# Rest of a feed-forward in two sweeps, the second with seven products of quarter blocks in place of eight

## The chip, the cores and the metric

The kernel runs on one core of a Trainium2 chip. The metric is device time in microseconds (us). Engines: PE does matrix products (PEld is its loading of weights), DVE vector work, ACT activations and copies, POOL elementwise work, SP issues most transfers. Matrix products write to PSUM, which has eight banks of 128 x 512 32-bit words; all else lies in SBUF.

## The reference

`B=8` batches, `S=576` positions, `DM=512` (8 heads of 64), hidden width 2048; 4608 tokens in all.

```python
kv  = einsum('bhsd,bhse->bhde', k, v); out = einsum('bhsd,bhde->bhse', q, kv)
x   = out / sqrt(mean(out*out, -1) + 1e-6) * g_norm        # heads side by side: (8, 576, 512)
u   = x + real(fft(fft(x, axis=1), axis=2))
un  = (u - mean(u, -1)) / sqrt(var(u, -1) + 1e-6)
out = u + maximum(un @ w_ch1, 0) @ w_ch2                   # w_ch1 512x2048, w_ch2 2048x512, 64-bit
```

## The kernel before, in words

All large products take 32-bit operands split into a high word that PE multiplies exactly and a low word that holds the rest; each product is three matmuls (`passes`): high x high, high x low, low x high. The weights come as 64-bit numbers; `sum_w` turns 512 columns of them into 32-bit values (one ACT operation, five on DVE and an addition), `split_w` makes the two words (ACT rounds, POOL subtracts), and for the first weights also takes each column's mean out through a small matmul (`w_mean`).

The tokens are 9 blocks (`NBLK`) of 512 (`BT`), each of 4 tiles of 128. The hidden width is 16 chunks f of 128. For a block and a chunk there are two halves of work. `ffn1` (L350 to L361): 12 matmuls, weights `w` of chunk f against the transposed tokens `unTh`, `unTl`, 512 columns each, into a bank `ps_h`; ACT takes the relu rounded (`hh`, L364), DVE the low word (`hl`, L367). `ffn2` (L369 to L378): for each of four tiles 3 matmuls of 512 columns, `hh` or `hl` against the second weights, summed over f in a bank `acc` per tile. A row's factor 1/sqrt(var) is the same for a whole token and positive, so it is left out of the hidden values and multiplied in at the end.

The program has two parts. Up to L1051 a planner (class `Plan`) emits attention, Fourier transform, norm and chunks f = 0 to 2 of the feed-forward, in order of ranks; the partial sums go to memory (`part_scr`), u to `u_scr`, the transposed tokens to `unT_scr`. From there on, the rest of the feed-forward is written out in program order, and a scheduler places the instructions of each engine in its queue. It works in steps of one block and one chunk: `first` of this step, then `second` of the step before (so 12 and 12 matmuls of 512 columns), and beside it one unit of weight conversion and the loads ahead (`load_unT`, two transfers of 1024 KB a block; `load_parts`, `load_u`). Four blocks first run f = 3 to 6, whose weights are ready, and store sums to `next_scr`; then all nine blocks run what is left, while the 18 weight units of f = 7 to 15 are converted, one a step. When a block is complete, `load_u` has computed the factors of its rows (`rs_yb`) and put u and the partial sums together in `uu`; DVE adds `acc` times the factor (L1186), and SP stores the tile (L1189).

Of the kernel before, what the change touches and what calls it, by code (L numbers as in the profile page):

```python
# [27 lines left out]
NA = 3  # L28
NB1 = 4
# [156 lines left out]
def kernel(  # L186
# [74 lines left out]
    part_scr = dram.tile([NTOK, DM], F32, name="part_scr")  # L261
    next_scr = dram.tile([NTOK, DM], F32, name="next_scr")
    unT_scr = dram.tile([NBLK, P, 2, KC * BT], F32, name="unT_scr")
# [82 lines left out]
    def h_tile(name):  # L346
        return base.tile([P, BT], F32R, name=name, tag="r", bufs=RINGS["h"])
# [487 lines left out]
    def plan_w(which, f, pool, r, after=(), r_load=None):  # L835
        pair = {}

        def make():
            pair["t"] = pool().tile([P, 2, BT], F32R, name=f"w{which}{f}", **(
                dict(tag="wA", bufs=2 * NA) if f < NA else {}  # L840
            ))
            w_t[which, f] = (pair["t"][:, 0], pair["t"][:, 1])
# [214 lines left out]
    def craw(name):  # L1057
        return wA.tile([P, 2 * DM], F32, name=name, tag="wA", bufs=2 * NA)

# [15 lines left out]
    def sum_w(which, f):  # L1075
# [9 lines left out]
        sums[which, f] = af, pf[:, :P]  # L1085

    def split_w(which, f):
# [5 lines left out]
        pair = wB2.tile([P, 2, BT], F32R, name=f"w{which}{f}")  # L1093
        hi, lo = w_t[which, f] = (pair[:, 0], pair[:, 1])
        nc.scalar.activation(hi, af, AF.Copy)  # L1095
        nc.gpsimd.tensor_tensor(lo, af, hi.bitcast(F32), ALU.subtract)  # L1096

    F1 = NA + NB1
    early = [NBLK - 2, NBLK - 1] + list(range(NBLK - 3, NBLK - 1 - NSEG, -1))
    blocks = early[::-1][: len(early) - 2] + early[:2] + list(range(1, NBLK - NSEG)) + [0]  # L1100
# [3 lines left out]
    tiles_of = {j: list(range(TPB)) for j in blocks}  # L1104
    tiles_of[0] = [2, 3, 0, 1]
    acc_t = {}
# [4 lines left out]
    def load_parts(j):  # L1111
        parts[j] = []
        for i in range(TPB):
            n = j * TPB + i
            two_ = []
            for src in (part_scr, next_scr)[: 2 if j in early else 1]:
                part = upool.tile([P, DM], F32, name="up", tag="up", bufs=6)
                nc.sync.dma_start(part, src[n * P : (n + 1) * P])
                two_.append(part)
            if j in early:  # L1120
                nc.gpsimd.tensor_tensor(two_[0], two_[0], two_[1], ALU.add)
            parts[j].append(two_[0])

    def load_u(j):
        us[j] = []
        mv = tiny.tile([P, TPB, 2], F32, name="bmv")
        for i in range(TPB):
            n = j * TPB + i
            ut = upool.tile([P, DM], F32, name="uu", tag="uu", bufs=8)
            if ascending(n):  # L1130
# [15 lines left out]
        for i in range(TPB):  # L1146
# [5 lines left out]
            nc.gpsimd.tensor_tensor(us[j][i], us[j][i], part, ALU.add)  # L1152

    held = [NBLK - 2, NBLK - 1]

# [7 lines left out]
    def first(j, f):  # L1163
        ps = bank("ps_h")
        ffn1(ps, w_t[1, f], unTs[j])
        hh, hl = h_tile("hh"), h_tile("hl")
        relu_hi(hh, ps)
        relu_lo(hl, ps, hh)
        return hh, hl

    def second(seg, hpair, f):
        j, f0, f1 = seg
        for i in tiles_of[j]:
            if f == f0:
# [4 lines left out]
            t = j * TPB + i  # L1179
            if f1 < NF:  # L1180
                part = upool.tile([P, DM], F32, name="up", tag="up", bufs=6)
                nc.scalar.copy(part, acc_t[i])
                nc.sync.dma_start(next_scr[t * P : (t + 1) * P], part)
                continue
            ut = us[j][i]
            nc.vector.scalar_tensor_tensor(  # L1186
                ut, acc_t[i], scales[j][:, i : i + 1], ut, ALU.mult, ALU.add
            )
            nc.sync.dma_start(out[t * P : (t + 1) * P, :], ut)  # L1189

    prev = None
    step = 0
    for n, seg in enumerate(segs):
        j, f0, f1 = seg
        for f in range(f0, f1):
            if step == 0:
                load_w(*units[0])
                load_w(*units[1])
            if step + 2 < len(units):
                load_w(*units[step + 2])  # L1200
            if f == f0 and n + 1 < len(segs) and segs[n + 1][0] not in held:
                load_unT(segs[n + 1][0], j)
            hpair = first(j, f)
            if prev:
                second(*prev)
            prev = (seg, hpair, f)
            if 0 < step <= len(units):
                split_w(*units[step - 1])
            if step < len(units):
                sum_w(*units[step])  # L1210
            step += 1
            if f == min(f0 + 2, f1 - 2):
                if f1 == NF:
                    load_parts(j)
                    load_u(j)
    second(*prev)
    late.close()
# [81 lines left out]
```

## Time and profile before

| | |
|---|---|
| median of 3 runs | 1027.12 us (1025.77 to 1027.71) |
| profiled execution | 1026.22 us, its span 1024.4 us |
| mean granted TensorE clock | 0.996 |
| busy: PE, PEld, DVE, ACT, POOL | 993.9, 839.4, 472.0, 322.4, 320.6 us |
| matmuls | 5866, of which 3456 at L354 and L372 have 512 columns |
| moved by transfers | 140.70 MB, 137 GB/s on average |

In a line of instructions the columns are: line, engine, operation, output <- inputs, shapes, count, then total busy time in us and the mean of one in ns, then the idle time of the engine just before them and what ended it. A busy share in a line of slices is given in tenths, 9 being 90% or more. Matmuls are pipelined: the mean of one is longer than the interval between two.

### The profile page before, as it was taken

What the parts mean: (1) busy time and instruction counts of PE and PEld (TensorE: products, weight loads), DVE (VectorE), ACT (ScalarE), POOL (GpSimd) and SP (SyncE); (2) the same over time, 40 slices, a digit from 0 to 9 for tenths busy, and PEclk for the clock granted to TensorE, in tenths of its full rate; (3) what the DMA queues carried; (4) which work ended last, traced back from release to release, by engine and by line L of the source; (5) the groups of instructions that cost most, each with busy time, mean ns of one, the idle gap of its engine ahead of it and who ended that gap; (6) DMA issues with size and microseconds to landing.
All of it is one profiled execution on the core that took longest, in us unless ns stands there. A gap on an engine that the chain in (4) does not pass through costs nothing.

```text
span 1024.4 us, 15026 instructions
## 1 busy us (share of the span) xinstructions
PE 993.9 (97%) x5866; PEld 839.4 (82%) x5866; DVE 472.0 (46%) x838; ACT 322.4 (31%) x655; POOL 320.6 (31%) x332
## 2 busy tenths in 40 slices
PE   4698999999999999999999999999999999999998
PEld 4697898889888888888888888888888888888886
DVE  4758775654588689998131314131221311311211
ACT  2456565555545434334221212021121021210110
POOL 0555876864865131225722303020020010110000
PEclk9998999999999999999999999999999999999999
DMA  9979979663246766645552515140320400400101
GB/s 245 253 164 280 190 214 263 168 182 139 88 162 212 275 206 253 228 136 175 155 177 74 182 51 170 71 139 1 125 81 0 165 21 1 164 1 1 42 1 41
DMA packets 109194, 140.70 MB, mean 137 GB/s; under 512 B 51790, under 2 KB 76418, under 8 KB 104516
## 3 DMA queue, kind: packets, MB, share of 16 engines
q1 hardware_dynamic: 105588, 132.28, 42.4%
q0 software_dynamic: 1920, 6.29, 2.0%
q10 hardware_dynamic: 1616, 1.18, 0.4%
q8 instruction: 46, 0.75, 0.3%
q14 instruction: 24, 0.20, 0.1%
HBM read 88.33 MB, written 51.40 MB: 136 GB/s over the span
## 4 chain that ended last, share of the span: by engine, by line
PE 93%; DMA 2%; DVE 2%; SPq 1%; issue 1%; ACT 0%; POOL 0%; DVEq 0%; ACTq 0%; POOLq 0%
PE ps_h L354 38%; PE acc L372 38%; PE ps_o L554 4%; PE ps_f L727 3%; PE ps_f L693 3%; PE ps_k L481 3%; PE ps_q L529 2%; PE ps_t L813 2%; DMA vm<-in_v_dram 2%; DVE x L651 1%; DMA qt<-in_q_dram 1%; SPq L510 1%; PE ps_w L315 0%; SPq L460 0%; DVE unTl L825 0%
## 5 line engine op out<-in xcount | busy, mean ns | idle before, releaser
L354 PE MATMUL ps_h<-unTh,w 128*128 128x512 f32 x1152 | 357.1, 391 | 0.0
L372 PE MATMUL acc<-w,hh 128*128 128x512 f32 x1152 | 345.0, 391 | 0.2 <-DVE unTl L825 0.2
L367 DVE SCALAR_TENSOR_TENSOR hl<-ps_h,hh 128x512 fp32r<-128x512 f32 x144 | 99.2, 689 | 379.8 <-ACT hh L364 377.5
L354 PEld LDWEIGHTS ps_h<-unTh,w 128*128 128x128 f32 x1152 | 215.4, 188 | 44.0
L372 PEld LDWEIGHTS acc<-w,hh 128*128 128x128 f32 x1152 | 214.9, 188 | 44.3 <-issue 0.3
L364 ACT ACTIVATE hh<-ps_h 128x512 fp32r<-128x512 f32 x144 | 85.9, 597 | 472.1 <-PE ps_h L354 442.9
L354 PE MATMUL ps_h<-unTl,w 128*128 128x512 f32 x576 | 224.5, 390 | 0.0
L372 PE MATMUL acc<-w,hl 128*128 128x512 f32 x576 | 213.1, 390 | 0.0
L354 PEld LDWEIGHTS ps_h<-unTl,w 128*128 128x128 f32 x576 | 108.3, 188 | 22.7
L372 PEld LDWEIGHTS acc<-w,hl 128*128 128x128 f32 x576 | 107.9, 188 | 22.5
L1133 POOL DMA_INDIRECT uu<-u_scr,rowidx x24 | 23.4, 974 | 286.2 <-DVE uu L1186 175.6
L589 POOL TENSOR_TENSOR x<-x,gb 96x512 f32<-96x512 f32 (+1 forms) x48 | 61.9, 1308 | 55.2 <-ACT x L569 40.6
L1152 POOL TENSOR_TENSOR uu<-uu,up 128x512 f32<-128x512 f32 x36 | 45.7, 1293 | 44.5 <-ACT up L1149 44.5
L554 PEld LDWEIGHTS ps_o<-kvt,fq 64*96 64x96 f32 (+1 forms) x768 | 42.7, 185 | 5.6 <-issue 3.2
L554 PE MATMUL ps_o<-kvt,fq 64*96 64x64 f32 (+1 forms) x768 | 47.0, 274 | 0.3 <-ACT fq L533 0.3
L481 PE MATMUL ps_k<-vm,km 128*64 128x64 f32 x512 | 28.7, 261 | 17.6 <-DMA vm<-in_v_dram 16.7
L1096 POOL TENSOR_TENSOR w<-wap,w 128x512 fp32r<-128x512 f32 x18 | 23.3, 1295 | 70.1 <-ACT w L1095 70.1
L1186 DVE SCALAR_TENSOR_TENSOR uu<-acc,rs_yb,uu 128x512 f32<-128x512 f32 x36 | 25.2, 745 | 42.5 <-PE acc L372 42.5
L578 DVE TENSOR_REDUCE ss<-ps_o 96x8 f32<-96x512 f32 (+1 forms) x48 | 32.2, 682 | 26.2 <-ACT ps_o L574 26.0
L669 POOL TENSOR_TENSOR xe<-ab 96x256 f32<-96x256 f32 (+1 forms) x48 | 37.5, 803 | 19.8 <-DVE ab L662 19.7
L693 PE MATMUL ps_f<-cs,xh 96*128 96x290 f32 (+1 forms) x192 | 41.8, 312 | 0.4 <-DVE x L651 0.4
L481 PEld LDWEIGHTS ps_k<-vm,km 128*64 128x64 f32 x512 | 22.9, 166 | 22.4 <-DMA km<-in_k_dram 16.2
(103 smaller groups left out, 1009.1 us busy)
## 6 DMA issues: line engine op xcount, KB each, us to landing
raw<-in_moe_w_ch_dram SPq DMA_DIRECT2D x32, 512.0 KB, 7.6
qt<-in_q_dram SPq DMA_DIRECT2D x16, 576.0 KB, 9.2
unT_scr<-unTh SPq DMA_DIRECT2D x9, 1024.0 KB
unT_scr<-unTl SPq DMA_DIRECT2D x9, 1024.0 KB, 6.3
part_scr<-part SPq DMA_DIRECT2D x36, 256.0 KB, 4.1
unTh<-unT_scr SPq DMA_DIRECT2D x9, 1024.0 KB, 4.9
unTl<-unT_scr SPq DMA_DIRECT2D x9, 1024.0 KB, 7.0
up<-part_scr SPq DMA_DIRECT2D x36, 256.0 KB, 3.0
```

Source lines behind the costliest of these rows:

```text
L354: nc.tensor.matmul(ps, w[c][:, kc * P : (kc + 1) * P], unT[a][:, kc, :], start=(idx == 0), stop=(idx == 3 * KC - 1),)
L364: nc.scalar.activation(hh, ps, AF.Relu)
L367: nc.vector.scalar_tensor_tensor(hl, ps, 0.0, hh.bitcast(F32), ALU.max, ALU.subtract)
L372: nc.tensor.matmul(acc, hpair[a][:, i * P : (i + 1) * P], w[c], start=(first and n == 0), stop=(last and n == 2),)
L481: nc.tensor.matmul(ps.t[s * D : (s + 1) * D, pr * D : (pr + 1) * D], km[:, s, j, :] if j < 4 else kr[:, h, :], vm[:, s, j, :] if j < 4 els ...
L554: nc.tensor.matmul(pss[s].t[:n, at : at + D], fqs[side].t[half, m, :n], kvt.t[half, m], start=True, stop=True,)
L578: nc.vector.tensor_reduce(ss.t[0][:n, :, t, s::2], pss[s].t[:n].rearrange("p (u m e) -> p u m e", u=2, e=D), AX.X, ALU.add,)
L589: nc.gpsimd.tensor_tensor(v_, v_, gb[:n].unsqueeze(1).to_broadcast([n, H, D]), ALU.mult)
L669: nc.gpsimd.tensor_tensor(o[:, s], a[:, 0], a[:, 1], ALU.subtract if s else ALU.add)
L693: nc.tensor.matmul(ps.t[:, :NS], xs[t].t[a][:n, part, ch * P : (ch + 1) * P], cs[:n, part, c, t, :], start=(idx == 0), stop=(idx == 8),)
L727: nc.tensor.matmul(ps.t[:n, :ND], pt.t[a][:, part, ch, offs[t] : offs[t] + n], cd[:, part, c, ch, :], start=(idx == 0), stop=(idx == 5),)
L1152: nc.gpsimd.tensor_tensor(us[j][i], us[j][i], part, ALU.add)
```

## The change

The hand-written part (from L1051) is replaced by two sweeps; the part under the planner stays.

**Sweep 1** takes all nine blocks through f = 3 to 7 (45 steps of 12 + 12 matmuls of 512 columns as before). At the end of each block DVE adds `acc` times the factor to u and the partial sums (L1186 as before), and the result goes to memory, `v_scr`. `store_scale` turns the block's factors from a column per tile into rows by a PE transpose (`ps_r`, L1183), an ACT copy and a store (`r_scr`). The weight units of f = 7 to 15 are spread over these steps.

**Sweep 2** takes all blocks again, in two halves of 256 tokens, through the pairs of chunks (8,9), (10,11), (12,13), (14,15): 9 x 2 x 4 = 72 steps. `firsts` makes the hidden values of both chunks for 256 tokens, 24 matmuls of 256 columns into one bank `ps_h`. `quarters` takes relu times the rows' factors (`r_scr` read back and spread over partitions, tile `part`), on DVE (L1320). The hidden values of a half are then a 2 x 2 matrix of 128 x 128 blocks a11, a12 (chunks) and a21, a22 (second tile), and the second weights of a pair are 2 x 2 blocks of 128 x 256, b11 to b22. Sums s1 to s4 of the a's (L1326 to L1329, s3 on POOL) and t1 to t4 of the b's (`split_pair`) give seven products in place of eight:

- a12·b21, a22·t4, a11·b11, s2·t2, s3·t3, s1·t1, s4·b22

`seven` makes them in that order, three matmuls of 256 columns each (L1352), and sums each over the four pairs in a bank of its own. ACT rounds a's and s's to high words (L1333), DVE makes the low words (L1334). After the fourth pair `gather` lets ACT copy the seven banks to SBUF (L1369) and adds them up into the two tiles of the half, eight adds on DVE and three on POOL (L1372, written into the following steps by the list `later`); the last half does it straight from PSUM (`gather_last`, L1398 and L1405).

```diff
-    F1 = NA + NB1
-    early = [NBLK - 2, NBLK - 1] + list(range(NBLK - 3, NBLK - 1 - NSEG, -1))
...
-    segs = [(j, NA, F1) for j in early]
-    segs += [(j, F1 if j in early else NA, NF) for j in blocks]
-    units = [(which, f) for f in range(F1, NF) for which in (1, 2)]
+    def split_pair(f):
+        b1, b2 = (sums.pop((2, f + i))[0] for i in range(2))
+        b11, b12, b21, b22 = b1[:, :QW], b1[:, QW:], b2[:, :QW], b2[:, QW:]
...
+        nc.vector.tensor_tensor(t1, b12, b11, ALU.subtract)
+        nc.vector.tensor_tensor(t2, b22, t1, ALU.subtract)
+        nc.gpsimd.tensor_tensor(t3, b22, b12, ALU.subtract)
+        nc.vector.tensor_tensor(t4, b21, t2, ALU.subtract)
...
+            nc.scalar.activation(hi, src, AF.Copy)
+            nc.gpsimd.tensor_tensor(lo, src, hi.bitcast(F32), ALU.subtract)
...
+    F1 = NA + NB1 + 1
+    sweep = [NBLK - 2, NBLK - 1] + list(range(NBLK - 3, -1, -1))
+    segs = [(j, NA, F1) for j in sweep]
+    again = [sweep[-2], sweep[-1]] + sweep[-3::-1]
...
+    def store_scale(j):
+        ps = bank("ps_r")
+        nc.tensor.transpose(ps[:TPB, :P], scales[j], ident)
+        row = tiny.tile([TPB, P], F32, name="brow", bufs=1)
+        nc.scalar.copy(row, ps[:TPB, :P])
+        nc.sync.dma_start(r_scr[j * TPB : (j + 1) * TPB], row)
...
-            nc.sync.dma_start(out[t * P : (t + 1) * P, :], ut)
+            nc.sync.dma_start(v_scr[t * P : (t + 1) * P], ut)
...
+    def firsts(j, half, f):
+        ps = bank("ps_h")
+        for i in range(2):
...
+            for kc in range(KC):
+                for a, c in passes:
+                    nc.tensor.matmul(
+                        ps[:, i * QW : (i + 1) * QW],
+                        w_t[1, f + i][c][:, kc * P : (kc + 1) * P],
+                        unTs[j][a][:, kc, half * QW : (half + 1) * QW],
...
+    def quarters(ps, j, half):
...
+        nc.vector.scalar_tensor_tensor(
+            h.rearrange("p (f t) -> p f t", f=2), ps.rearrange("p (f t) -> p f t", f=2), 0.0,
+            r.unsqueeze(1).to_broadcast([P, 2, QW]), ALU.max, ALU.mult,
+        )
+        a11, a21, a12, a22 = (h[:, i * P : (i + 1) * P] for i in range(4))
+        s1, s2, s3, s4 = (s[:, i * P : (i + 1) * P] for i in range(4))
+        nc.vector.tensor_tensor(s1, a21, a22, ALU.add)
+        nc.gpsimd.tensor_tensor(s3, a11, a21, ALU.subtract)
+        nc.vector.tensor_tensor(s2, s1, a11, ALU.subtract)
+        nc.vector.tensor_tensor(s4, a12, s2, ALU.subtract)
...
+            nc.scalar.activation(hi, src, AF.Copy)
+            nc.vector.tensor_tensor(lo, src, hi.bitcast(F32), ALU.subtract)
...
+    def seven(j, half, f, left):
...
+        for a, b in products:
+            if f == F1:
+                sums_t[a] = bank("acc")
+            for n, (x, y) in enumerate(passes):
+                nc.tensor.matmul(
+                    sums_t[a][:, :QW], left[a][x], w_q[f][b][y],
+                    start=(f == F1 and n == 0), stop=(last and n == 2),
+                )
...
+    def gather(j, half):
...
+        for pair in (("a12", "a22"), ("a11", "s1"), ("s2", "s3"), ("s4",)):
+            zt = upool.tile([P, DM], F32, name="up", tag="up", bufs=6)
...
+                nc.scalar.copy(z[a], sums_t[a][:, :QW])
...
+        later.extend([
+            [
+                add(pool, l0, z["a11"]), add(pool, l0, z["a12"]),
+                add(vec, z["s2"], z["a11"]), add(vec, z["s3"], z["s2"]), add(vec, r0, z["s2"]),
+            ],
+            [add(pool, l1, z["a22"]), add(vec, l1, z["s3"]), add(vec, r1, z["s3"])],
+            [add(vec, z["s4"], z["s1"]), add(vec, r1, z["s1"]), add(vec, r0, z["s4"])],
+            [out_(0, v0), out_(1, v1)],
+        ])
...
+                ps = firsts(j, half, f)
+                if prev:
+                    prev()
+                left = quarters(ps, j, half)
+                prev = lambda a=(j, half, f, left): seven(*a)
...
+                if later:
+                    for go in later.pop(0):
+                        go()
```

Three places in the queues of the engines, as the two programs have them. First DVE, over the last two blocks before the change (`hl`: low words of the relu; `uu`: output tiles):

```order
L367 SCALAR_TENSOR_TENSOR hl<-ps_h,hh 128x512 x10
L1186 SCALAR_TENSOR_TENSOR uu<-acc,rs_yb,uu 128x512
L367 SCALAR_TENSOR_TENSOR hl<-ps_h,hh 128x512
L1186 SCALAR_TENSOR_TENSOR uu<-acc,rs_yb,uu 128x512 x3
L367 SCALAR_TENSOR_TENSOR hl<-ps_h,hh 128x512 x12
L1186 SCALAR_TENSOR_TENSOR uu<-acc,rs_yb,uu 128x512 x4
```

and DVE after the change at the end of a half block, from the scaled relu (`hs`) of the next half's first step to that of its second (`ss`: s1 to s4; `both`: high and low words; `up`: the copied products):

```order
L1320 SCALAR_TENSOR_TENSOR hs<-ps_h,part 128x512
L1326 TENSOR_TENSOR ss<-hs 128x128
L1328 TENSOR_TENSOR ss<-ss,hs 128x128
L1329 TENSOR_TENSOR ss<-hs,ss 128x128
L1334 TENSOR_TENSOR both<-hs,both 128x512
L1372 TENSOR_TENSOR up<-up 128x256 x2
L1372 TENSOR_TENSOR uu<-uu,up 128x256
L1334 TENSOR_TENSOR both<-ss,both 128x512
L1372 TENSOR_TENSOR uu<-uu,up 128x256 x2
L1372 TENSOR_TENSOR up<-up 128x256
L1372 TENSOR_TENSOR uu<-uu,up 128x256
L1320 SCALAR_TENSOR_TENSOR hs<-ps_h,part 128x512
```

Where a chunk had one DVE instruction and a block's end four, seven of the eight adds of `gather` now stand between two of the L1320.

Second, ACT at the same place after the change; before, it had only the relus of L364 there:

```order
L1369 COPY up<-acc 128x256 x2
L1333 ACTIVATE both<-hs 128x512
L1369 COPY up<-acc 128x256 x3
L1333 ACTIVATE both<-ss 128x512
L1369 COPY up<-acc 128x256 x2
L1333 ACTIVATE both<-hs 128x512
```

The copies are those of a12 and a22, then a11, s1 and s2, then s3 and s4; between them stand the two roundings of the next half's first step.

Third, PE around such a place with its waits, from the last products of the first step to the hidden chunk two steps on (`q`: words of the combined weights; the number after a name tells tiles apart):

```order
L1352 MATMUL acc<-q_5198,both 128x256 [waits Activation_49]
L1352 MATMUL acc<-q_5198,both 128x256 x2
L1305 MATMUL ps_h<-unTh,w_5723 128x256 [waits DVE_49]
L1305 MATMUL ps_h<-unTh,w_5723 128x256
L1305 MATMUL ps_h<-unTl,w_5723 128x256
```

Before, PE's queue had 12 matmuls of L354 and 12 of L372 by turns, all of 512 columns. Now 24 of L1305 and 21 of L1352 take turns, and since seven banks hold products, the first L1305 waits for DVE's L1320 of the step before it, which empties the eighth.

More of the change, by code (lines that the diff above doesn't have):

```diff
@@ L1114, in load_parts @@
             n = j * TPB + i
[L1115 to L1122, printed above, removed]
+            part = upool.tile([P, DM], F32, name="up", tag="up", bufs=6)
+            nc.sync.dma_start(part, part_scr[n * P : (n + 1) * P])
+            parts[j].append(part)
     def load_u(j):
@@ L1209 @@
-            if step < len(units):
-                sum_w(*units[step])
-            step += 1
[L1212 to L1216, printed above, removed]
+            do_work(step, (load_w,))
+            if f == f0 and order_of[n + 1] not in held:
+                load_unT(order_of[n + 1], j)
+            hpair = relu(first(j, f))
+            if prev:
+                prev()
+            prev = lambda a=(seg, hpair, f): second(*a)
@@ L1217 @@
+    prev()
+    for group in later:
+        for go in group:
+            go()
     late.close()
```

171 lines of the change are left out of this document (144 added, 27 removed).

## The prediction

> **What bounds the kernel now.** I read the page's busy shares, its forty slices and its chain first, then one window over the stage that changes. These are the busy times, the PE slices and the chain's shares by engine.
>
> ```profile
> PE 993.9 (97%) x5866; PEld 839.4 (82%) x5866; DVE 472.0 (46%) x838; ACT 322.4 (31%) x655; POOL 320.6 (31%) x332
> PE   4698999999999999999999999999999999999998
> PE 93%; DMA 2%; DVE 2%; SPq 1%; issue 1%; ACT 0%; POOL 0%; DVEq 0%; ACTq 0%; POOLq 0%
> ```
>
> PE is 97% busy and 93% of the chain. Its dips lie in the first seven slices, which the change leaves as they are. In the stage that changes, the window from the last weight conversion to the last hidden chunk reads (engines as PE, PEld, DVE, ACT, POOL; then clock, DMA share, GB/s):
>
> ```profile
> 499.84:1013.92 514.08, 514.08 (x2270) 425.68 (x2269) 113.51 (x217) 77.52 (x129) 63.64 (x55) 1.00 0.23 77
> ```
>
> PE never rests, at full clock, and 514.08/2270 = 226.5 ns pass per 128x512 matmul. DVE is 22% busy, ACT 15%, POOL 12%. So here the time is the number of matmuls times their interval, and the change can gain only there; it can lose wherever another engine makes PE wait.
>
> **Removed and added on PE.** 72 steps of 24 matmuls of 512 columns become 72 steps of 24+21 = 45 matmuls of 256. The old step is 24 x 226.5 ns = 5.44 us. No matmul of this kernel is 256 wide; the nearest are those of L727 (258 columns) and L693 (290). From the chain (start, us, matmuls), the timeline, and the lines of L727 and L813:
>
> ```profile
> 226.02 4.30 PE ps_f L727 x36
> 123.66 4.33 PE ps_f L727 x36
> 244.89 4.84 PE ps_f L693 x36
> L727 PEld LDWEIGHTS ps_f<-cd,pt x288: 159/162/166, 71.8 to 324.5; 128*96 128x96 f32 x94, 128*97 128x97 f32 x50
> 320.20 4.46 PEld L727 LDWEIGHTS ps_f<-cd,pt 128*97 128x97 f32 x36
> L813 PEld LDWEIGHTS ps_t<-ident,x x192: 137/140/144, 78.4 to 338.8; 96*128 96x128 f32 x128, 97*128 97x128 f32 x32, 95*128 95x128 f32 x32
> 337.01 2.15 PE L813 MATMUL ps_t<-ident,x 97*128 97x97 f32 x24
> ```
>
> 4.30 to 4.33 us for 36 are 119.4 to 120.3 ns; two columns fewer, at (226.5 - 119.4)/(512 - 258) = 0.42 ns a column, make 118.6 to 119.5. The 290-wide row (134.4 ns) comes to 120.2. I take 119.0, nearer to the 258-wide rows: 45 x 119.0 = 5.355 us, 0.085 less than the old step, and 72 x 0.085 = **-6.1 us** (bounds: 118.6 ns gives -7.4, 120.2 gives -2.2). The loads do not lengthen this: 36 of 162 ns each went through in 4.46 us, and 128-column ones of 140 ns passed with their matmuls every 2.15/24 = 90 ns. Nine small transposes of the scales at those 90 ns add **+0.8**.
>
> The Trainium skill ("TensorE: Matmul & The Clock Gate", "Wait — 56ns, not 53.3ns?") puts a warm matmul at N/2.4 plus about 2.5 ns; an estimate from it is 215.8 ns for 512 and 109.2 for 256, which would save 72 x 0.265 = 19 us. The trace does not agree: the surplus is 226.5 - 213.3 = 13.2 ns at 512 columns and 119.4 - 107.5 = 11.9 at 258, so most of the surplus is paid per matmul, and halving the width pays it twice. The measurement decides.
>
> **Moved: the work behind each product.** In an ordinary step of the second sweep, DVE has five kinds of work: a scaled relu of 512 columns, three 128-column sums and two 512-column low words. Rows for sizes, from the lines and the timeline:
>
> ```profile
> 467.35 1.29 DVE L292 TENSOR_SCALAR ps_a<-ps_a 128x512 f32<-128x512 f32 x2
> L367 DVE SCALAR_TENSOR_TENSOR hl<-ps_h,hh 128x512 fp32r<-128x512 f32 x144 | 99.2, 689 | 379.8 <-ACT hh L364 377.5
> L710 DVE TENSOR_TENSOR pt<-ps_f,pt 128x290 fp32r<-128x290 f32 x32 | 13.9, 452 | 6.7 <-ACT pt L706 6.3
> L492 ACT COPY kvt<-ps_k 128x256 f32<-128x256 f32 x8 | 3.0, 376 | 12.2 <-PE ps_k L481 12.2
> L1095 ACT ACTIVATE w<-wap 128x512 fp32r<-128x512 f32 x18 | 11.5, 636 | 12.9 <-DVE wap L319 12.8
> L669 POOL TENSOR_TENSOR xe<-ab 96x256 f32<-96x256 f32 x32 | 24.1, 773 | 0.8 <-DVE ab L662 0.7
> L312 POOL TENSOR_TENSOR wp<-wp,wa 128x128 f32<-128x128 f32 x8 | 3.7, 461 | 0.6
> L1096 POOL TENSOR_TENSOR w<-wap,w 128x512 fp32r<-128x512 f32 x18 | 23.3, 1295 | 70.1 <-ACT w L1095 70.1
> ```
>
> Two DVE operations of 0.69 us passed in 1.29, so a queued one takes 0.60. From 0.69 at 512 columns and 0.45 at 290, at 0.0011 us a column, 256 columns take 0.42 alone and 0.33 queued, 128 take 0.19 queued. An ordinary step asks 0.60 + 3 x 0.19 + 2 x 0.60 = 2.4 of DVE's 5.36 us: it lies beside PE and costs nothing. The combinations of weights (split_pair, four times) are 1792 columns to round and subtract: POOL, the slowest there, needs 3.5 x 1.295 + 0.77 = 5.3 us, and the last pair has four steps (21 us) until its use, so this costs nothing either; without that cover it would be those 5.3 us once.
>
> At the end of each half block (17 times before the last) it is tight. Seven of the eight PSUM banks hold products, so one is left for ps_h, and PE may start the hidden chunk two steps on only when DVE's L1320 has read the one in between. From the end of one hidden chunk to that point PE has 21 + 24 + 21 = 66 matmuls, 7.85 us; a weight load a matmul ahead leaves 7.73. What stands before that L1320 in DVE's queue waits for ACT: up to the end of the copy of s3 are six copies and two roundings, 6 x 0.376 + 2 x 0.636 = 3.53 us, and the first product closes at 3 x 0.119 = 0.36, so DVE can go on at 3.9 after having waited. Then come six 256-column adds (1.95), one low word (0.60) and L1320 itself (0.69): ready at **7.15**, with 0.6 to spare.
>
> POOL's three adds, though, run in that stretch. The trace shows what DVE pays for such company: its adds with both inputs in SBUF (L662) take 672 ns at best and 3962 at worst.
>
> ```profile
> L662 DVE TENSOR_TENSOR ab<-x x24: 672/682/3962, 44.1 to 301.2; 96x512 f32<-96x512 f32 x16, 97x512 f32<-97x512 f32 x8
> 119.88 3.60 POOL L669 TENSOR_TENSOR xe<-ab 97x256 f32<-97x256 f32 x4 [3.69 <-DVE ab L662]
> 121.67 1.21 DVE L662 TENSOR_TENSOR ab<-x 96x512 f32<-96x512 f32 x1 [0.60 <-POOL xe L669]
> 189.13 5.41 DVE L662 TENSOR_TENSOR ab<-x 96x512 f32<-96x512 f32 x2
> 190.07 1.64 POOL L757 TENSOR_TENSOR x<-x,pm 96x514 f32<-96x514 f32 x1
> 191.66 1.18 POOL L760 TENSOR_TENSOR x<-x,pm 96x510 f32<-96x510 f32 x1
> 192.80 1.19 POOL L757 TENSOR_TENSOR x<-x,pm 96x514 f32<-96x514 f32 x1
> ```
>
> The add at 121.67 took 1.21 us, 0.53 over its 0.68, beside 256-wide POOL work like the new one; the pair at 189.13 took 5.41, through three POOL operations on end. If the two engines shared nothing, DVE would be ready at 7.15 and the stall is 0. If they took strict turns from 2.1 us on (a11's copy out, POOL's first add), both queues are one: 0.60 + 0.33 + 1.95 + 0.60 + 0.69 of DVE and 3 x 0.773 of POOL, 6.5 us, ready at 8.6, a stall of 0.87. Taking the 0.53 of the row for one or two of the three adds (the first fits into DVE's wait for ACT) gives 7.7 to 8.2; I take 7.88, the middle of both ends, a stall of 0.15: 17 x 0.15 = **+2.5** (bounds 0 and 14.8).
>
> **Sweep 1** now stores sums and scales and reloads everything twice. Rows for its traffic: a full window and the loads.
>
> ```profile
> 391.68:491.68 100.00, 100.00 (x450) 83.06 (x449) 86.71 (x144) 41.40 (x73) 34.47 (x27) 1.00 0.55 189
> 364.00:372.17 8.17, 8.17 (x38) 1.00 0.85 266
> raw<-in_moe_w_ch_dram SPq DMA_DIRECT2D x32, 512.0 KB, 7.6
> unTh<-unT_scr SPq DMA_DIRECT2D x9, 1024.0 KB, 4.9
> up<-part_scr SPq DMA_DIRECT2D x36, 256.0 KB, 3.0
> ```
>
> A block of five steps takes 27.2 us and moves 2 MB of unT, 1 MB each of parts, u and stored sums, and one ninth of 18 weights of 0.5 MB: 6 MB, 220 GB/s. A share of 0.85 went with 266 GB/s, so 0.70 of the queues. DVE at 87% kept PE full, and converts no denser now. New on PE's queue is the transpose, which waits for u's statistics, loaded two steps (10.9 us) before. I put **+0.5** (0 to +8).
>
> **The end.** Timeline of the old one:
>
> ```profile
> 1018.29 1.07 PE L372 MATMUL acc<-w,hl 128*128 128x512 f32 x4
> 1018.78 2.73 DVE L1186 SCALAR_TENSOR_TENSOR uu<-acc,rs_yb,uu 128x512 f32<-128x512 f32 x4 [3.51 <-PE acc L372]
> 1019.56 2.31 SPq L1189 DMA_DIRECT2D out_dram<-uu  x4
> ```
>
> DVE ends 2.15 us after PE. The new end has nine DVE adds of 0.42 for seven products closing every 0.36: they start with the first product, 2.14 before PE ends, and with one more wait for ACT and POOL end some 2.4 after it. I take **+0.3** (-0.7 to +1.5).
>
> **Sum:** -6.1 + 0.8 + 2.5 + 0.5 + 0.3 = -2.0. The profiled execution took 1026.22 us (span 1024.4 and 1.8 around it), so 1024.2; the median of the runs, 1027.12, is 0.9 above it, so **1025.1**. From no change, 0.2% (2.05 us) can be told: 1025.07 is where faster begins, 1029.17 where slower does.
>
> **Rivals.** (B) *The half-block ends cost nothing*: POOL's adds fit into DVE's waits, and sweep 1 is clean. For it: 0.6 us to spare, DVE 22% busy. Against: the 0.53 of the row. -6.1 + 0.8 + 0.3 = -5.0: 1022.1.
>
> (C) *DVE loses the shared port to POOL at each half-block end*, as in the row of 5.41 us, and PE waits 0.5 us (between 0.15 and 0.87) 17 times: -6.1 + 0.8 + 0.5 + 0.3 + 8.5 = +4.0, 1031.1, slower. It decides from (6.1 - 1.6 + 2.05)/17 = 0.39 us a time. Against: in the row of 121.67 DVE came in after one operation. By the Trainium skill ("SBUF — State Buffer", "Who interferes with whom") a DVE instruction with two SBUF inputs contends with GpSimd's reads for a shared pair, held for a whole instruction; the 3962 ns agree.
>
> (D) *Sweep 1 waits*: a transpose or a block's first chunk waits some 0.7 us in each of nine blocks for u or unT, with the queues at 0.70: +6 in place of +0.5, so +3.5, 1030.6. Against: at 0.85 PE still had no gap.
>
> (E) *The interval goes by columns alone*: 226.5/2 = 113.3 ns, 45 of them 5.10 us, -24.5 in place of -6.1: 1006.7. Against it stand the 258-wide rows.
>
> **How the numbers follow.** My own case has 0.46, B 0.22, C 0.21, D 0.09, E 0.02. My case reaches from a stall of 0 to 0.35 with the PE bounds, 1022.5 to 1028.5 or so; its middle is at the border, so 0.23 of it is faster, 0.20 the same, 0.03 slower. B and E are faster; of C 0.18 and of D 0.07 are slower, the rest the same. Faster 0.47, same 0.25, slower 0.28. The range 1020.5 to 1033 leaves out E, the far part of C and D and the lowest of B, some 0.15.
>
> **What would show it.** In the changed profile: L1305 and L1352 at 119 ns each; the time from the first to the last of them 72 x 5.36 = 386 us plus the stalls; 17 idle times of PE before L1305, put down to DVE hs L1320, of 0.15 us each; DVE's L1372 longer than 0.42 when POOL's L1372 runs; few idle times before L1183. An interval off 119 by 1 ns is worth 3.2 us and would make the prediction wrong by itself, as would a stall above 0.4 us or a gap in every block of sweep 1.

## The result

The changed kernel takes 1039.61 us (median of 4 runs, 1039.16 to 1041.6) against 1026.44 us for the kernel before, run beside it (4 runs, 1025.07 to 1027.71): 1.0132 times as long, 95% interval 1.0112 to 1.0152. It is slower by 13.2 us; 1025.1 had been predicted, with a range up to 1033. The profiled execution took 1039.96 us, its span is 1038.2.

Its page, first busy times, then the slices of PE, of the clock and of the transfers, then the chain by engine:

```profile
PE 1001.1 (96%) x7387; PEld 909.1 (88%) x7387; DVE 719.3 (69%) x1355; ACT 399.3 (38%) x848; POOL 402.1 (39%) x453
PE   5798999999999999989899999999999999999997
PEclk9998999999999999989999999999999999999999
DMA  9969688563336686655675531232232422314001
PE 87%; DMA 6%; DVE 4%; SPq 1%; issue 1%; ACT 1%; POOL 0%; DVEq 0%; ACTq 0%; POOLq 0%
```

PE's busy time is 7 us more, not less. Its slices dip at 441 to 467 and at 493 to 519 us, the granted clock in the first of these; transfers now have 6% of the chain where they had 2%. The loss is easiest to read if both programs are cut at the same matmuls: where PE starts on the 36 matmuls L373 (L372 before) at 338 us, the end of sweep 1 (before: after the same number of 512-wide matmuls), and the last one. These are the windows of the changed kernel and of the one before (columns as in the prediction):

```profile
338.32:638.23 299.91, 292.00 (x1279) 239.80 (x1278) 205.49 (x379) 95.81 (x173) 107.83 (x95) 0.98 0.59 205
638.23:1032.14 393.91, 393.91 (x3254) 392.01 (x3252) 287.21 (x579) 125.44 (x269) 91.41 (x128) 1.00 0.26 91
```

```profile
339.48:624.80 285.32, 285.32 (x1271) 236.55 (x1269) 162.76 (x284) 85.88 (x151) 84.17 (x73) 1.00 0.52 178
```

| stretch, us, of the profiled executions | before | changed | difference |
|---|---|---|---|
| to the start of the cut (the same instructions) | 339.5 | 338.3 | -1.2 |
| sweep 1 | 285.3 | 299.9 | +14.6 |
| from there to the start of the last matmul | 394.2 | 393.8 | -0.4 |
| from there to the end of the span | 5.4 | 6.2 | +0.7 |

So the second sweep, for which the change was costed, is a draw, and the first sweep, costed at half a microsecond, is the loss. There PE is idle for 299.91 - 292.00 = 7.9 us. Where, the chain of waits of the changed kernel tells around the first dip (start, us, what):

```profile
438.37 4.60 DMA v_scr<-uu
443.00 6.77 DMA uu<-u_scr,rowidx
449.79 0.69 DVE bst L1167
451.19 0.02 ACT rs_sb L327
451.31 0.59 ACT hh L365
451.94 3.78 PE acc L373 x8
```

A block's sum must be stored (4.60 us) before the slot of `uu` is free; only then does the load of a later block's u begin (6.77 us); DVE waits for it with the row statistics (`bst`), ACT waits with the square root of the variance (`rs_sb`), and behind that, in ACT's queue, stands the rounded relu (`hh`) of a chunk that has long been computed; PE waits for that. The second gap, 4.4 us up to 515.28, has the same chain: a store of 9.06 us, a load of u of 4.29, the statistics, then a sum of weights behind them (`wap`, L308), for which PE's `ps_w` waits. The groups of waits say it again (waiting line, releaser, us in all, times, longest; ACT from 430 to 455 us, DVE from 430 to 640, PE from 340 to 645):

```profile
ACT rs_sb L327 <- DVE bm L1171: 10.1, 1, 10.1
DVE bst L1167 <- DMA uu<-u_scr,rowidx: 19.6, 6, 6.6
PE ps_w L316 <- DVE wap L308: 4.4, 1, 4.4
PE acc L373 <- ACT hh L365: 3.4, 1, 3.4
```

Before the change DVE waited for u at the same statistics (L1140), in more and shorter pieces (340 to 1024 us), and PE had no gap:

```profile
DVE bst L1140 <- DMA uu<-u_scr,rowidx: 17.9, 17, 1.9
DVE bst L1140 <- DMA uu<-u_scr: 8.7, 4, 3.0
```

What is waited for is not even urgent. By the order of loads, statistics and sums in the trace, loads and statistics run ahead of their use by as much as the ring allows: the statistics that DVE begins at 449.79 us belong to a block whose sum comes at 497.9, those at 512.05 to one summed at 531.9.

And after each of the two gaps the clock is not at full:

```profile
451.94:458.70 6.76, 6.76 (x18) 5.45 (x19) 6.69 (x15) 3.65 (x6) 2.21 (x2) 0.54 0.01 2
515.28:519.61 4.33, 4.33 (x13) 3.47 (x14) 4.33 (x13) 0.64 (x2) 0.00 (x0) 0.61 0.02 6
```

The time lost is the window times what the clock lacks: 6.76 x 0.46 + 4.33 x 0.39 = 4.8 us. In the trace's clock record these are two pieces at half, 6.8 us from 451.34 (0.6 us before the gap ends) and 3.4 us from 516.20 (0.9 us after PE has begun again); inside them 512-wide matmuls follow each other at 427 ns for 227. With 7.9 us of idle PE and nine transposes of 0.11 that is 13.7 of the 14.6. The Trainium skill ("TensorE: Matmul & The Clock Gate", "What's actually happening") has two clock states, the lower after an idle window of some 3.4 us. The gaps of 3.4 and 4.4 us here agree; a later run (experiment 4) had half clock after a gap of 2.7 us, so 3.4 us is not a floor for the gap.

### The profile page after: what moved, and what is told of

The parts are those of the page before. It is cut to its first block, busy times and chain, and to the rows that moved or that the text cites. A ratio compares the mean times of both kernels' runs of the same rounds, so it can differ in the third digit from the quotient of the medians.

```text
span 1038.2 us, 19213 instructions
## 1 busy us (share of the span) xinstructions
PE 1001.1 (96%) x7387; PEld 909.1 (88%) x7387; DVE 719.3 (69%) x1355; ACT 399.3 (38%) x848; POOL 402.1 (39%) x453
## 4 chain that ended last, share of the span: by engine, by line
PE 87%; DMA 6%; DVE 4%; SPq 1%; issue 1%; ACT 1%; POOL 0%; DVEq 0%; ACTq 0%; POOLq 0%
PE ps_h L1305 20%; PE acc L1352 17%; PE ps_h L355 16%; PE acc L373 16%; PE ps_o L555 4%; PE ps_f L694 3%; PE ps_f L728 3%; PE ps_k L482 3%; PE ps_q L530 2%; PE ps_t L814 2%; DMA uu<-u_scr,rowidx 2%; DMA v_scr<-uu 2%; DMA vm<-in_v_dram 1%; DMA uu<-u_scr 1%; DVE x L652 1%
## 5 line engine op out<-in xcount | busy, mean ns | idle before, releaser
L1305 PE MATMUL ps_h<-unTh,w 128*128 128x256 f32 x1152 | 212.2, 284 | 0.0
L1352 PE MATMUL acc<-q,both 128*128 128x256 f32 x1512 | 193.3, 283 | 0.0
L1352 PEld LDWEIGHTS acc<-q,both 128*128 128x128 f32 x1512 | 186.7, 192 | 0.1
L355 PE MATMUL ps_h<-unTh,w 128*128 128x512 f32 x576 | 182.8, 398 | 0.0
L1305 PEld LDWEIGHTS ps_h<-unTh,w 128*128 128x128 f32 x1152 | 179.4, 192 | 1.5 <-DVE hs L1320 0.4
L373 PE MATMUL acc<-w,hh 128*128 128x512 f32 x576 | 174.3, 396 | 3.7 <-ACT hh L365 3.4
L1305 PE MATMUL ps_h<-unTl,w 128*128 128x256 f32 x576 | 163.0, 283 | 0.0
L373 PEld LDWEIGHTS acc<-w,hh 128*128 128x128 f32 x576 | 107.4, 190 | 26.3 <-ACT hh L365 4.3
L355 PEld LDWEIGHTS ps_h<-unTh,w 128*128 128x128 f32 x576 | 108.6, 191 | 22.7
L355 PE MATMUL ps_h<-unTl,w 128*128 128x512 f32 x288 | 113.6, 394 | 0.0
L1305 PEld LDWEIGHTS ps_h<-unTl,w 128*128 128x128 f32 x576 | 110.5, 192 | 0.0
L1333 ACT ACTIVATE both<-hs 128x512 fp32r<-128x512 f32 x72 | 45.6, 633 | 158.0 <-DVE hs L1320 154.6
L373 PE MATMUL acc<-w,hl 128*128 128x512 f32 x288 | 105.4, 391 | 0.0
L1320 DVE SCALAR_TENSOR_TENSOR hs<-ps_h,part 128x512 f32<-128x512 f32 x72 | 49.7, 690 | 57.3 <-PE ps_h L1305 57.3
L1334 DVE TENSOR_TENSOR both<-ss,both 128x512 fp32r<-128x512 f32 x72 | 49.7, 690 | 41.4 <-ACT both L1333 41.4
L1333 ACT ACTIVATE both<-ss 128x512 fp32r<-128x512 f32 x72 | 45.5, 632 | 63.5 <-DVE ss L1329 63.5
L373 PEld LDWEIGHTS acc<-w,hl 128*128 128x128 f32 x288 | 53.9, 188 | 11.4
```

The costliest lines, as they stand in the source:

```text
L355: nc.tensor.matmul(ps, w[c][:, kc * P : (kc + 1) * P], unT[a][:, kc, :], start=(idx == 0), stop=(idx == 3 * KC - 1),)
L373: nc.tensor.matmul(acc, hpair[a][:, i * P : (i + 1) * P], w[c], start=(first and n == 0), stop=(last and n == 2),)
L1305: nc.tensor.matmul(ps[:, i * QW : (i + 1) * QW], w_t[1, f + i][c][:, kc * P : (kc + 1) * P], unTs[j][a][:, kc, half * QW : (half + 1) * QW ...
L1320: nc.vector.scalar_tensor_tensor(h.rearrange("p (f t) -> p f t", f=2), ps.rearrange("p (f t) -> p f t", f=2), 0.0, r.unsqueeze(1).to_broad ...
L1333: nc.scalar.activation(hi, src, AF.Copy)
L1334: nc.vector.tensor_tensor(lo, src, hi.bitcast(F32), ALU.subtract)
```

## The experiments

Theory A: the gaps come from u's slot, passed on by the queues of DVE and ACT. Theory C: a matmul has a fixed part, so that 256 columns cost more than half of 512, and seven products of half the width gain next to nothing. Against them stand traffic (B) and the quarter products with their sums as the cause (D, E).

**1. u in an idle ring.** One of a block's four u tiles goes to the ring `part`, which nothing uses in sweep 1.

```diff
-            ut = upool.tile([P, DM], F32, name="uu", tag="uu", bufs=7)
+            if i == 0 and j != sweep[-1]:
+                ut = part_tile()
+            else:
+                ut = upool.tile([P, DM], F32, name="uu", tag="uu", bufs=7)
```

> The changed kernel; only one of the four u tiles of a block in sweep 1 (all blocks but the last) lies in the ring named part, which is idle there, so that a block asks three of the seven uu slots, not four, and none of its loads waits for the previous block's sum to be stored. Theory A (slots): the gaps in sweep 1 (7.9 us of PE idle, 10.2 us at half clock after them, 5.1 us of loss) come from this wait, passed on by the queues of DVE and ACT that stand behind the row statistics: 13 us go, 1026 to 1028 us, sweep 1 (from 338 us to the first L1305) 285 to 287 us instead of 300, second sweep as it is. Rival B (traffic): the queues at 0.6 to 0.7 make u late whatever slot it has: within 3 us of the changed kernel, 1037 to 1040.

1029.2 us (10 runs, 1025.69 to 1032.78), 1.0027 of before (1.0011 to 1.0043): 10.4 us less than the changed kernel. Sweep 1 of the profiled execution, the slowest of the ten:

```profile
340.63:631.46 290.83, 287.70 (x1279) 236.37 (x1278) 203.95 (x381) 97.23 (x176) 110.36 (x98) 1.00 0.61 212
```

290.8 us in place of 299.9, the clock at 1.00, with the same transfers (212 GB/s, more than before). That is A's way and not B's: u's indirect loads even took longer to land, 6.2 us in the median for 5.4 in the changed kernel (3.5 before the change), so slow transfers alone do not make the loss. It falls short of the 285 to 287: 3.1 us of idle PE remain, at places where DVE and ACT still stand behind the statistics. DVE's waits for u from 400 to 630 us fell only from 30.9 to 24.2 us; with the slot, the statistics also took other places in DVE's queue (the first at 395.3 us for 380.2), and the runs do not separate the two.

**2. The second sweep as before the change.** Products of 512 columns, one chunk at a time, seven slots.

```diff
-        at(s + every * 3 + 1, split_pair, f)
...
-                ps = firsts(j, half, f)
-                left = quarters(ps, j, half)
+            hpair = relu(first(j, f))
+            prev = lambda a=(seg, hpair, f): second2(*a)
```

> The changed kernel with its first sweep (seven uu slots), and a second sweep as before the change: blocks of 512 tokens, f = 8 to 15 one at a time, 12 + 12 matmuls of 512 columns, no sums of quarters, no scaled rows (the factor is kept and multiplied at the end; the nine transposes and stores of factors are left out). Theory A with C (a 256-wide matmul takes 120.0 ns, so 45 of them cost 5.40 us against 5.44): the second sweep lasts 391 us as in the changed kernel and the loss is sweep 1's: 1036 to 1040 us. Rival D (the products of quarters with their sums are what costs): 1026 to 1029 us.

1040.59 us (4 runs), 1.0141 (1.0104 to 1.0178). The sum was just above what A and C had, but for another reason: sweep 1 had one gap, of 0.8 us, and no half clock. In the second sweep a window holds fewer matmuls than the same window before the change (there, 442), although PE never rests:

```profile
700.00:800.00 100.00, 100.00 (x438) 82.04 (x438) 17.71 (x26) 10.77 (x18) 0.00 (x0) 1.00 0.24 84
```

In its first sweep the median interval was 232 ns for 227. A new tile of 144 bytes had moved all tiles behind it to addresses 32 bytes off a multiple of 64. So it was made again with that tile at 512 bytes, which puts the others back, and the offset was tried by itself:

> The run with the plain second sweep again (seven uu slots), with the same instructions and one tile of 144 bytes made 512 bytes, so that all tiles behind it start at multiples of 64 bytes as in the changed kernel and the kernel before; there they started 32 bytes off, and its 512-wide matmuls took 232 ns in sweep 1 and 228.7 on average in the second, 227 elsewhere. If the offset is the reason: 226.7 ns throughout. Then, by the theory of slots, sweep 1 has the gaps of the changed kernel: 1036 to 1040 us; if the gaps need the weight combinations, transposes and stores of the full change as well: 1027 to 1030 us.

> The kernel before the change, instruction for instruction, with one padding tile of 64 bytes in place of 32, so that the tiles behind it (tokens, hidden values, weights) start 32 bytes off a multiple of 64. Theory G (an operand 32 bytes off costs PE): 512-wide matmuls of the hand-written part take 228 to 233 ns, 6 to 18 us more in all, 1032 to 1045 us. Rival: the slow intervals of the plain second sweep came from its transfers or its order: 1026.5 us, no change.

The aligned one took 1036.42 us (4 runs), 1.009 (1.0065 to 1.0115), and its sweep 1 is that of the changed kernel, with gaps of 3.3 and 3.2 us and half clock behind both:

```profile
339.19:636.36 297.17, 290.65 (x1270) 239.64 (x1269) 199.17 (x377) 92.20 (x160) 98.18 (x86) 0.98 0.60 206
```

Its second sweep took 394.2 us, as before the change, and as the changed one's 393.8. So the loss is there without any product of quarters: D falls. The kernel before with 32 bytes of offset took 1033.85 us (5 runs), 1.0065 (1.0043 to 1.0088), with the same instructions in the same order: theory G holds. From 400 to 490 us it got through 397 matmuls, the one before through 407:

```profile
400.00:490.00 90.00, 90.00 (x397) 73.07 (x396) 80.73 (x128) 37.59 (x66) 26.75 (x21) 1.00 0.58 199
```

**3. Twelve slots.** The aligned run, with room for twelve `uu` tiles in place of seven.

```diff
-            ut = upool.tile([P, DM], F32, name="uu", tag="uu", bufs=7)
+            ut = upool.tile([P, DM], F32, name="uu", tag="uu", bufs=12)
```

> The aligned run with the plain second sweep (1036.4 us), instruction for instruction in what it computes, with twelve uu slots in place of seven (a plain second sweep leaves room for them), so that u's loads wait for stores of two or three blocks back and never for the previous block's. Theory A (slots): its two gaps in sweep 1 (3.5 and 3.3 us of idle PE with 6.8 and 3.4 us of half clock behind them, 13.0 us over 227 ns a matmul in all) go, 1026 to 1029 us. Rival B (traffic): the transfers are the same, so u comes as late: 1034 us or more.

1031.71 us (6 runs), 1.0063 (1.0039 to 1.0087), 4.7 less than with seven. Sweep 1 is 289.2 us, both episodes of half clock are gone:

```profile
340.74:629.91 289.17, 286.12 (x1270) 236.27 (x1269) 205.47 (x378) 92.68 (x160) 101.95 (x87) 1.00 0.61 213
PE ps_w L316 <- DVE wap L308: 2.5, 1, 2.5
```

8.0 of the 11.9 us that sweep 1 had lost went with the slots alone, 3.5 of them idle time of PE and 4.5 half clock. Neither the 1026 to 1029 of A nor the 1034 of B was met: in the profiled execution one gap of 2.5 us is left, with no half clock behind it. Its timeline:

```profile
446.60 0.69 DVE L1168 BATCH_NORM_STATS2 bst<-uu 128x6 f32<-128x512 f32 x1 [2.42 <-DMA uu<-u_scr,rowidx]
448.93 5.46 POOL L1181 TENSOR_TENSOR uu<-uu,up 128x512 f32<-128x512 f32 x4 [4.13 <-ACT up L1178]
449.63 0.70 DVE L1168 BATCH_NORM_STATS2 bst<-uu 128x6 f32<-128x512 f32 x1 [1.58 <-DMA uu<-u_scr,rowidx]
450.24 1.77 DVE L303 SCALAR_TENSOR_TENSOR wap<-raw,wap 128x512 f32<-128x512 uint32 x1
451.94 1.26 DVE L1174 COPY keep<-rs_yb 128x4 f32<-128x4 f32 x1
```

DVE waits 2.4 and 1.6 us for u, and then two of its operations last 1.77 us (0.68 alone) and 1.26 us, for a copy of four columns, beside POOL's four additions; a sum of weights behind them comes late for PE. The copy is one that only the runs with a plain second sweep have, to keep the factors. And the loads did not come free of the stores, as the expectation had it: with twelve slots they run three blocks ahead and again begin when a store lands (442.6 to 444.2 us, behind the stores issued at 438.8 to 441.4), and DVE stands at the statistics of a block that is summed at 524.2. So more room takes away the larger part of the loss, and the queue behind the statistics remains.

**4. Loads earlier, statistics later.** On the run of experiment 1.

```diff
-            if f == f0 + 2:
-                load_parts(j)
-                load_u(j)
+            if f == f0 + 1:
+                load_u(j)
+                load_parts(j)
+            if f == f0 + 3:
+                rows_u(j)
```

> As the run with u in the idle ring, and in sweep 1 the loads of u and of the partial sums are issued one step earlier (behind the second chunk of a block, not the third) and the row statistics are placed one step later (behind the fourth chunk). That run still lost some 5.4 us of PE's time in sweep 1 beside the transposes, at four places where DVE's statistics waited for u with the low words, the sums of weights and the copies of others behind them. If this queueing is what is left: sweep 1's excess falls from 6.4 to 1 or 2 us and the run takes 1024 to 1026 us, 4 or 5 less. If the transfers are late for other reasons (full queues): 1028 to 1030 us, no change.

In the profiled execution sweep 1 falls to 287.5 us, 2.2 above the kernel before:

```profile
338.55:626.03 287.48, 286.81 (x1279) 236.46 (x1278) 204.74 (x381) 97.66 (x176) 110.60 (x98) 1.00 0.61 214
```

The median does not follow: 1028.76 us (12 runs, 1024.96 to 1030.88), 1.0017 (1.0002 to 1.0032), 0.4 less than experiment 1, which these runs cannot tell from nothing, and within the 1028 to 1030 of "no change". The profiled execution itself took 1027.32. How large the rest of sweep 1's waits is differs from run to run; a single trace does not settle it. The same first sweep was put before the plain second one:

> The aligned run with the plain second sweep, with u in the idle ring, loads of u one step earlier and row statistics one step later: two sweeps with 512-wide matmuls throughout and no gaps in sweep 1. Theory: two sweeps by themselves cost 1 or 2 us (what is left of sweep 1's waits), 1027 to 1029 us; no half clock after 100 us; and it equals the run with the same first sweep and seven products within 2 us, which says that these products gain nothing at 256 columns. Rival: splitting in two sweeps costs more than its gaps (traffic, 164 MB for 141): 1031 us or more.

1031.15 us (12 runs, 1027.38 to 1035.9), 1.0047 (1.003 to 1.0064). In its profile sweep 1 took 291.0 us, with a gap of 2.7 us and 3.4 us of half clock, again behind the statistics. That is the rival's time: two sweeps cost more, in this form and with its added copy, than the theory had it. In the chain of this gap a store of 6.3 us from the ring `part` comes first and then a load of u of 6.3, so u's way is the cause again; its slot and the amount of traffic were not separated further. The seven products stand 2.4 us better than this run, with the waits of sweep 1 differing by as much, so no gain or loss of theirs can be read from the two medians.

**5. Eight products.** On experiment 1, without sums s and t.

```diff
-    def seven(j, half, f, left):
+    def eight(j, half, f, left):
+        for t in range(2):
+            for c in range(2):
+                for i in range(2):
+                    a = ("a11", "a12", "a21", "a22")[2 * t + i]
```

> As the run with u in the idle ring, with all eight products of quarters and none of the sums (no s, no t, four sums in four banks, DVE adds them): 48 matmuls of 256 columns a step. Theory C (a fixed part of some 13 ns a matmul, whatever its width): 72 x 48 x 0.120 = 415 us for the second sweep, 26 more than with seven products, 1050 to 1054 us. Rival E (120.0 ns come from operands being made late, a plain 256-wide matmul costs half of 226.5): 72 x 48 x 0.1133 = 391.5 us, 1027 to 1030 us.

1051.08 us (4 runs), 1.0245 (1.0223 to 1.0267): theory C, 22 us more than with seven. In 100 us:

```profile
700.00:800.00 100.00, 100.00 (x836) 100.00 (x835) 31.33 (x54) 10.89 (x18) 0.00 (x0) 1.00 0.29 101
```

Matmul starts are 120 ns apart throughout (the count takes in those that overlap the window's ends), with DVE 31% busy and no operand late: 120.0 ns is what a 256-wide matmul costs here. 512 columns cost 226.5, so 256 more columns cost 106.5 ns, 0.416 each, and 13.5 of the 120.0 ns do not go by columns. The 290-wide row of the prediction lies on the same line (134.2 ns worked out, 134.4 read). The loads of weights are 100% busy in this window, 83% with 512 columns; that they set part of the 120 ns is not ruled out by a run of its own, only made unlikely by that line. Going from 512 to 256 columns costs 72 x 48 x 0.120 - 72 x 24 x 0.2265 = 23 us; the eighth product saves 72 x 3 x 0.120 = 26; what is left is 2.6 us.

**6. POOL's adds left out.** On experiment 4, one execution; the outputs lack what these adds bring.

```diff
-                add(pool, l0, z["a11"]), add(pool, l0, z["a12"]),
...
-            [add(pool, l1, z["a22"]), add(vec, l1, z["s3"]), add(vec, r1, z["s3"])],
+            [add(vec, l1, z["s3"]), add(vec, r1, z["s3"])],
```

> The run with the early loads and seven products; POOL's three adds at each half-block end are left out (the outputs lack a11, a12 and a22). In the changed kernel PE waits 0.10 us, twice 0.135 more, at the second hidden chunk after each half-block end, some 2 us in all. If POOL's hold on DVE's second operand makes DVE late: the waits go, the second sweep is 2 us shorter. If it is DVE's own chain behind ACT's copies: they stay at 0.10.

The waits at the half-block ends vanish. The second sweep to the start of the last matmul takes 391.7 us, for 393.4 with POOL's adds, and none of these adds on DVE is longer than 425 ns. In the changed kernel the adds on DVE beside them read (min/median/max in ns):

```profile
L1372 DVE TENSOR_TENSOR uu<-uu,up x85: 414/418/426, 667.9 to 1018.4; 128x256 f32<-128x256 f32 x85
L1372 DVE TENSOR_TENSOR up<-up x51: 416/426/959, 666.5 to 1017.1; 128x256 f32<-128x256 f32 x51
```

17 of the 51, one a half block, take 955 to 959 ns in place of some 420, 0.54 more, which is the 0.53 of the prediction's row.

**7. Hidden chunks of 512 tokens.** Theory C says what to do: only the seven products need 256 columns. The hidden chunks are made for a whole block again (12 matmuls of 512), the second half's values are kept until its products come, and products run five chunks behind.

```diff
-                ps = firsts(j, half, f)
+            ps = first(j, f)
...
+            seven(*seconds[m], left_of.pop(seconds[m]))
...
+            scaled(ps, j, i, [hs_of[j, half, f - i] for half in range(2)])
...
+            left_of[key] = quarters(hs_of.pop(key), s_ring[(m + 1) % 2])
```

> As the run with u in the idle ring, but the hidden chunks are made 512 tokens at a time (12 matmuls of 512 columns each), and only the seven products have 256 columns; the hidden values of a block's second half are kept (32-bit, five tiles) until its products come. One chunk and one set of products take turns, products five chunks behind. Theory C: 72 x (12 x 0.2265 + 21 x 0.120) = 377.1 us against 388.8, so 11.7 us less than that run, 1014 to 1018 us, faster than both kernels. Rival F: with one bank left, each chunk of hidden values waits for DVE to read the one before within the 2.5 us of the products: 0.2 to 0.4 us 72 times, 14 to 29 us, 1029 us or more.

1024.92 us (10 runs), 0.9982 (0.9969 to 0.9994). Faster than both kernels, by far less than the 1014 to 1018. The second sweep was 388.4 us in place of 393.4. F did not come as written (0.22 us at each block end, not 0.3 at each chunk), but 4.2 us went at the very end, where only products remain and wait for their words, and sweep 1 still lost 5. Both were changed: the loads and statistics of experiment 4, and words made two sets ahead.

```diff
-        if 0 <= m + 1 < len(seconds):
-            key = seconds[m + 1]
+        if 0 <= m + 2 < len(seconds):
+            key = seconds[m + 2]
```

> The run with 512-token hidden chunks, with the two changes of sweep 1 of the other run of this group, and the words of each set of products made one turn sooner (two sets ahead, products six chunks behind). The run before it lost 6.4 us in sweep 1, 1.8 at block ends and 4.2 at the end, where products alone remain and wait for their words. Queueing theory: 5 us less in sweep 1, 2 or 3 less at the end: 1017 to 1019 us. If the words are made no sooner because DVE and not the order is the limit at the end: 1019 to 1021 us.

1016.66 us (6 runs, 1014.32 to 1019.63), **0.9904** of before (0.9881 to 0.9926). Its two stretches:

```profile
339.92:627.40 287.48, 286.95 (x1279) 236.50 (x1278) 204.12 (x381) 97.59 (x176) 110.56 (x98) 1.00 0.61 214
627.40:1009.00 381.60, 381.28 (x2390) 345.80 (x2388) 277.48 (x647) 121.74 (x265) 91.52 (x125) 1.00 0.26 94
```

The second is 12.6 us shorter than the 394.2 before the change. A further change of sweep 1 puts the loads behind a block's first chunk:

> The faster run with 512-token hidden chunks, with the loads of u and partial sums issued one more step earlier, behind the first chunk of a block; statistics stay. Sweep 1 still lost 3.2 us there, of which some 1 us is the transposes. If what is left is u's way: 1 or 2 us less, 1015 to 1016 us. If not, the same 1016 to 1017 us.

1018.77 us (6 runs, 1016.48 to 1023.04), 0.9933 (0.9911 to 0.9956): no gain, though the profiled execution, the fastest of the six (1016.48), has sweep 1 at 286.4 us.

## Why the prediction was wrong

By its own terms, for the profiled execution, in us:

| term | predicted | measured | how |
|---|---|---|---|
| 45 matmuls for 24 | -6.1 (-7.4 to -2.2) | -2.6 | 120.0 ns each, 72 x (5.436 - 5.40) |
| transposes of scales | +0.8 | +1.0 | nine of 0.11 |
| half-block ends | +2.5 (0 to 14.8) | +2.2 | waits of PE in sweep 2: 17 of 0.10, two of 0.135, the rest 0.02 or less |
| sweep 1 | +0.5 (0 to 8) | +13.6 | 14.6 less the transposes |
| the end | +0.3 (-0.7 to 1.5) | +0.7 | 6.2 against 5.4 |
| first part | 0 | -1.2 | same instructions |
| sum | -2.0 | +13.7 | the rounded spans, 1038.2 - 1024.4, give 13.8 |

**The step that failed is sweep 1**: "I put +0.5 (0 to +8)". The parts for it were there: 0.70 of the queues, statistics that wait for u. But the argument asked whether PE's own instructions, the transposes, would wait for u. They never did (no wait before L1183 in the trace). Those that waited were DVE and ACT, with the relus and weight sums of other chunks queued behind the statistics. Rival (D) had the sweep and the sign right, but placed some 0.7 us at "a transpose or a block's first chunk" in each of nine blocks; what came were two gaps of 3.4 and 4.4 us, by another mechanism. And the argument took "DVE at 87% kept PE full" as proof that the queue had room: it was full of work, where now it stood still.

Of the edit of the ring from eight tiles to seven nothing was said at all. A block uses four, so with eight a load waits for the store two blocks back, with seven one of four waits for the block just finished; two blocks are ten chunks here where they had been 18 to 26. Eight to seven was in the diff, and costing it at nothing named no work that hides it. The trace bears this count out for the second gap, where the last tile of a block had to wait for the block just before it. The load at the first gap waited for the store two blocks back, as it would have with eight; before the change such loads (522.5 to 528.1 us, behind the stores of 520.5 to 523.3) cost PE nothing. With more room the medians of experiments 1 and 3 are 10.4 and 4.7 us lower, half clock included. The changed kernel with eight slots was not run, so how much of the loss is the one slot, and how much the place of the statistics in the queue, stays open.

**The bound was too low because a gap costs twice.** The bound of 8 was made from waits alone; half clock behind two gaps added 4.8. Before the change PE had no gap in this stretch, so the earlier trace did not show it.

**PE's saving** was mis-sized by one nanosecond: 119.0 was scaled from rows of 258 columns whose single intervals scatter, most of them from 114 to 125 ns, and the 290-wide row, with 120.2 kept as the bound, was the better one. The text named the price (1 ns, 3.2 us). Another 0.3 us came from rounding the old step, 24 x 226.5 ns = 5.436 us, to 5.44. To go by the measured surplus was right: 13.5 ns of a matmul do not go by its columns.

**Right** were the half-block ends, in mechanism and size: L1320 came just too late there, and leaving POOL's adds out removed it (0.18 us left of some 2.0). That the size fits so well is partly luck, as 7.88 was only the middle of two bounds. Rival C did not decide, at 0.10 a time for 0.39 needed. E is refuted by 120.0.

## What to carry to other kernels

When a block gets shorter, count every ring again in blocks, and follow what stands behind a waiting instruction on its own queue, not only who needs its result: here DVE and ACT, waiting for a load that was needed tens of microseconds later, held back work that had nothing to do with it. A gap on PE of some 3 us or more was paid a second time in clock. Before trading one product in eight for narrower matmuls, take the interval at both widths: with some 13 ns fixed for each, seven at 256 columns only broke even, and the gain came when what could stay at 512 stayed there.

## What the runs showed of the hardware that was not expected

- Operand tiles 32 bytes off a multiple of 64: part of the 512-wide matmuls at 231 to 236 ns for 227, with instructions and order unchanged; 0.65% (0.43 to 0.88) of this kernel. The offset came from a small tile far ahead in the same memory.
- 13.5 ns of a matmul's interval did not go by its columns (120.0 ns at 256, 134.4 at 290, 226.5 at 512), so they are paid per instruction here. At half clock they do not show: 427 ns for 512 columns is 0.83 a column, twice the 0.416 of full clock, with nothing left over.
- Half clock came in pieces of 6.8 and 3.4 us, after PE gaps of 3.4 and 4.4 us (the longer piece after the shorter gap). In sweep 1 of all these runs every gap of 2.7 us or more had one behind it, and none up to 2.5 us.
- The first 340 us, whose instructions are the same in all these programs, ended between 337.6 and 342.4 us in the profiled executions (the latest of them had 6.8 us at half clock at 107 us), so single executions differ by some microseconds before the changed part begins.
